# A fused attention and ELU feed-forward kernel: in the last step of a pair of heads, a copy of a product's bank goes ahead of the exponential

## The chip, the cores and the metric

The kernel runs on one core of one Trainium2 chip. The metric is the device time of one execution in microseconds. The kernel before was timed in six runs: median 1384.58 us, from 1382.22 to 1386.93. The engines are named as in the profile: PE is TensorE's matmul, PEld its weight load, DVE VectorE, ACT ScalarE, POOL GpSimd, SP SyncE, which issues the DMAs.

## The reference

Thresholded attention over 8 sequences, 8 heads, 576 positions of 64 values, in fp32, and then a feed-forward block with an ELU over the 4608 tokens.

```python
scores = scale * np.matmul(q, k.transpose(0, 1, 3, 2))          # (8, 8, 576, 576)
thresh = np.max(scores, axis=-1, keepdims=True) - tau
scores = np.where(scores >= thresh, scores, -1000000000.0)
attn = np.exp(scores - np.max(scores, axis=-1, keepdims=True))
attn = attn / (np.sum(attn, axis=-1, keepdims=True) + 1e-09)
x = np.matmul(attn, v)                                          # then to (4608, 512)
h = x @ w_in                                                    # (4608, 2048)
g = np.where(h > 0.0, h, np.exp(np.minimum(h, 0.0)) - 1.0)
out = g @ w_out                                                 # (4608, 512)
```

## The kernel before

The work is cut into 32 pairs of heads (8 sequences, 4 pairs each), and each pair into five steps. Steps 0 to 3 (`i < NC`, `NC` is 4) take 128 query rows of both heads; the fifth, `i == NC`, takes the last 64 rows of both heads together, as one set of 128 rows, so that it has a single score tile where the others have two. The attention of one sequence runs while the feed-forward products of an earlier one fill PE.

There are four stages. The first two attend the first sequence and the next pairs while weights are converted and a plain feed-forward runs. The third and longest is the loop at L1155 that this case is about: 115 steps, 23 pairs. What is left of the feed-forward runs after it with no attention beside it.

In the third stage the order on each engine is written out by an agenda: `at(t, f)` puts a job at a planned time `t`, `on_pe(cost, f)` runs all jobs that are due, then issues a piece of PE work and moves the planned clock on by its cost. The planned times are not run times; they only set the order in which instructions stand in each engine's queue. What waits for what is left to semaphores.

One step (`softmax`, L1115) starting at planned time `t`:

- scores (L238) on PE at once, one PSUM tile for each head, from two buffers;
- `max_of` (L1085, DVE) at `t + 1.2`: the row maximum `mx`;
- `bound_of` (L1089, POOL) at `t + 2.0`: the threshold `th`;
- `exp_of` (L1093 and L1095, both ACT) at `t + 2.1`: a scaled maximum `nb`, then the exponential `e`;
- `mask_of` (L1104, DVE): `e` where the score reaches the threshold, and the row sums; then the reciprocal (L1111, DVE) and the scaling of each head (L274, POOL);
- the transposition of the step before (L348 and L358, DVE, in 32 by 32 squares), which goes to DRAM and comes back two steps later by DMA (L361, L369);
- in steps 1 and 4, the product with the values of an earlier step (L384, L388, PE) and its copies (L395, L400, ACT).

Between these go quarters of the feed-forward (`ffn_quarters`). Both of its matrix products are done by a scheme with seven smaller products where eight would be plain. The first product (`first_product`, L846) has for one unit seven quarters `k = 0..6`, each of two fp32 matmuls, which the profile shows as four. They use three PSUM banks in turn, by `place`: `k = 0` and `3` and `6` write place 0, `k = 1` and `4` place 1, `k = 2` and `5` place 2. `k = 3`, `4`, `5` and `6` add to what is there. Between, ACT copies the banks out: after `k = 0`, `1` and `2` (L860) and after `k = 3` (L912) and `k = 4` (L913). L912 reads place 0, and `k = 6` then adds into place 0, so `k = 6` waits for L912. POOL adds some of the copies (L865), DVE adds the last two results to them (L868), and the ELU follows: an exponential on ACT (L879), minus one on ACT (L884) or POOL (L893), and DVE's L901. Four units make half a group; then the second product (`second_round`, L1001) reads the ELU's output and sums of it that POOL makes (L938).

A pair whose steps carry four units of the first product is followed by one that carries a second round: a round of the loop is two pairs, ten steps. In a first-product pair the fifth step is followed by the last four quarters (`k = 3..6`) of its fourth unit (`QUARTERS[4]` is `(4, 0)`). Line numbers up to L1122 are the same before and after the change.

Of the kernel before, what the change touches and what calls it, by code (L numbers as in the profile page):

```python
# [19 lines left out]
def kernel(  # L20
# [15 lines left out]
    NC = S // P  # L36
# [132 lines left out]
    def load(pr, parts=("qm", "km", "v"), shared=False):  # L169
        b, j = divmod(pr, NPAIR)  # L170
        tiles = raws.setdefault(pr, {})
        for name, src in (("qm", q), ("km", k)):
            if name not in parts:
                continue
            m = tiles[name] = raw.tile([P, S // T, T], FP32, name="qm" if shared else name)
            for i in range(2):
                for d in range(2):
                    r = (2 * i + d) * T
                    nc.sync.dma_start(
                        m[r : r + T],  # L180
                        src[b, 2 * j + i].rearrange("(j t) d -> t j d", t=T)[:, :, d * T : (d + 1) * T],
                    )
        if "v" not in parts:
            return
        vm = tiles["vm"] = raw.tile([P, 2, NC, D], FP32, name="vm", bufs=2)
        vd = tiles["vd"] = vds[pr % NVD]
        for i in range(2):
            vh = v[b, 2 * j + i]
            nc.sync.dma_start(vm[:, i], vh[:MAIN].rearrange("(c p) d -> p c d", p=P))
            r = slice(i * TAIL, (i + 1) * TAIL)  # L190
            nc.sync.dma_start(vd[r, r], vh[MAIN:])
# [30 lines left out]
    def scores(pr, i, hs):  # L222
        qT, kT, qd = pairs[pr]
        if hs[0] == 0:
            open_steps[pr, i] = {
                **{x: small.tile([P, 2], FP32, name=x) for x in ("mx", "nb", "th", "sm", "rs")},
            }
        st = open_steps[pr, i]
        if "f" in psum and not apart:
            both = psum["s"].tile([P, 2, 2, 512], FP32, name="sc")  # L230
            scs = {h: both[:, h] for h in hs}
        else:
            scs = {h: psum["s"].tile([P, 2, 512], FP32, name="sc") for h in hs}
        for a in range(2):
            for h in hs:
                k0 = a * HALF + (0 if h else TAIL)
                r, qs = (slice(h * D, (h + 1) * D), qT[:, i * P : (i + 1) * P]) if i < NC else (slice(0, P), qd)
                nc.tensor.matmul(scs[h][:, a, :HALF], qs[r], kT[r, k0 : k0 + HALF], start=True, stop=True)  # L238
        if len(hs) == 2 and not apart:
            st["both"] = both  # L240
        for h in hs:
            st[h] = scs[h]
# [27 lines left out]
    def normalize(pr, i, hs):  # L270
        st = open_steps[pr, i]
        for h in hs:
            wv = st["w"][:, h * S : (h + 1) * S]
            nc.gpsimd.tensor_scalar(wv, wv, st["rs"][:, h : h + 1], 1.0, ALU.mult, ALU.mult)  # L274
# [68 lines left out]
    def turn_squares(pr, i):  # L343
        w = open_steps.pop((pr, i))["w"]
        x = late["x"].tile([P, NT, NCH, T], FP32, name="x", bufs=2)

        def turn_part(c0, src, nc_):
            nc.vector.transpose(x[:, :, c0 : c0 + nc_], src.rearrange("p (c g n) -> p g c n", c=nc_, n=T))  # L348

        if i < NC:  # L350
            turn_part(0, w[:, :MAIN], NC)
            turn_part(NC, w[:, MAIN : MAIN + P], 1)
            turn_part(NC + 1, w[:, MAIN + P :], NC)
        else:
            turn_part(0, w[:, :MAIN], NC)
            turn_part(NC + 1, w[:, :MAIN], NC)
            for h in range(2):
                nc.vector.transpose(x[:, 2 * h : 2 * h + 2, NC], w[:, MAIN:S].rearrange("p (g n) -> p g n", n=T))  # L358
        there = turns[pr, i] = dram.tile([NT, T, NT, NCH * T], FP32, name="there")
        for p in range(NT):  # L360
            nc.sync.dma_start(  # L361
                there[:, :, p].rearrange("c k n -> k c n"), x[p * T : (p + 1) * T].rearrange("k c j n -> k c (j n)")
            )
# [48 lines left out]
    def run_extra(budget):  # L412
        while extra and extra[0][0] <= budget:
            cost, _, f = extra.popleft()
            budget -= cost
            f()
# [89 lines left out]
    def heads_of(i):  # L506
        return [0, 1] if i < NC else [0]
# [83 lines left out]
    with tc.manual_schedule():  # L591
# [3 lines left out]
        for n in range(per_seq, SWITCH):  # L595
            pr, i = step = steps[n]
# [149 lines left out]
    with tc.manual_schedule():  # L746
        after = []
        make_out(1), make_out(0)
        for n in range(SWITCH, MIDDLE):
            pr, i = steps[n]  # L750
# [46 lines left out]
        def at(t, f):  # L797
            serial[0] += 1
            heapq.heappush(agenda, (t, serial[0], f))
# [9 lines left out]
        def on_pe(cost, f):  # L809
            until(clock[0])  # L810
            f()
            clock[0] += cost
            return clock[0]
# [139 lines left out]
        def run_elus(t):  # L953
            while late_elus and late_elus[0][0] < t - 1.5:
                late_elus.pop(0)[1]()
# [127 lines left out]
        def max_of(pr, i, h):  # L1083
            st = open_steps[pr, i]
            nc.vector.tensor_reduce(st["mx"][:, h : h + 1], st[h][:, :, :HALF], axis=AX.XY, op=ALU.max)  # L1085

        def bound_of(pr, i, h):
            st = open_steps[pr, i]
            nc.gpsimd.tensor_scalar(st["th"][:, h : h + 1], st["mx"][:, h : h + 1], 1.0, ntau, ALU.mult, ALU.add)  # L1089

        def exp_of(pr, i, h):
            st = open_steps[pr, i]
            nc.scalar.mul(st["nb"][:, h : h + 1], st["mx"][:, h : h + 1], nkeep)  # L1093
            e = att.tile([P, 2, HALF], FP32, name="e")
            nc.scalar.activation(e, st[h][:, :, :HALF], AF.Exp, bias=st["nb"][:, h : h + 1], scale=keep)  # L1095
            st[h] = st[h], e

        def mask_of(pr, i, h):
            st = open_steps[pr, i]
            if h == 0:  # L1100
                st["w"] = wpool[0].tile([P, 2 * S], FP32, name="w")
            sc, e = st.pop(h)
            wv = st["w"][:, h * S : (h + 1) * S].rearrange("p (a n) -> p a n", a=2)
            nc.vector.scalar_tensor_tensor(wv, sc[:, :, :HALF], st["th"][:, h : h + 1], e, ALU.is_ge, ALU.mult,  # L1104
                                           accum_out=st["sm"][:, h : h + 1])

        def reciprocal_of(pr, i, hs):
            st = open_steps[pr, i]
            cs = slice(hs[0], hs[-1] + 1)
            nc.vector.tensor_scalar(st["sm"][:, cs], st["sm"][:, cs], 1e-9, None, ALU.add)  # L1110
            nc.vector.reciprocal(st["rs"][:, cs], st["sm"][:, cs])  # L1111
# [3 lines left out]
        def softmax(pr, i):  # L1115
            hs = heads_of(i)
            t = begun[0] = clock[0]
            on_pe(1.25, lambda: scores(pr, i, hs))
            turn_at = t + 1.25 + 0.72 * len(hs)
            for h in hs:  # L1120
                at(t + 1.2 + 0.01 * h, lambda h=h: max_of(pr, i, h))
                at(t + 2.0 + 0.75 * h, lambda h=h: bound_of(pr, i, h))  # L1122
                at(t + 2.1 + 1.05 * h, lambda h=h: exp_of(pr, i, h))
                at(turn_at + 1.6 + 0.85 * h, lambda h=h: mask_of(pr, i, h))
            if i or pr:
                at(turn_at, lambda: turn_squares(*steps[pr * NB + i - 1]))
            m = turn_at + 1.6 + 0.85 * len(hs)
            at(m, lambda: reciprocal_of(pr, i, hs))
            at(m + 0.1, lambda: run_elus(m))
            for h in hs:  # L1130
                at(m + 0.2 + 0.7 * h, lambda h=h: normalize(pr, i, [h]))
            for x in (2.8, 3.8, 5.0):
                at(t + x, lambda: run_extra(max(0.9, extra[0][0])) if extra else None)
            if pr + 1 < NP and i in (0, 2):
                at(m + 0.2, lambda: (prep_k if i else prep_q)(pr + 1))
                at(m + 1.3, lambda: (copy_k if i else copy_q)(pr + 1))

            if pr + 1 < NP and i == 0 and pr * NB > MIDDLE:
                at(m + 0.9, lambda: load(pr + 1, ("km",), True))
            if pr + 2 < NP and i == 2:  # L1140
                at(m + 0.9, lambda: load(pr + 2, ("qm",), True))
            if pr + 1 < NP and i == 3:
                at(m + 0.9, lambda: load(pr + 1, ("v",)))
# [11 lines left out]
        for n in range(MIDDLE, len(steps) + 3):  # L1155
            pr, i = divmod(n, NB)
# [116 lines left out]
```

## Time and profile before

| What | Value |
|---|---|
| median of six runs | 1384.58 us |
| the profiled execution: its time, its span | 1382.77 us, 1380.6 us |
| mean granted clock of TensorE | 0.992, and 1.00 in the loop |
| matmul PE, busy over the span | 97% |
| DVE, ACT, POOL, busy over the span | 77%, 45%, 60% |
| the third stage | about 316 to 1150 us |
| one round of it (ten steps) | 72.75 us |
| mean of one L1095, L912, L913 | 831, 364, 372 ns |
| mean of one L1085, L1104, L274 | 752, 811, 860 ns |

The profile is one execution. "Busy" of PE counts modelled ends of pipelined matmuls: matmuls that follow each other at 0.22 us are shown with some 0.38 us each. In a timeline, a row is a start and a duration in microseconds, the engine, the line, the operation, the tiles out and in, and the form; in brackets stand the idle time of the engine before it and what ended that. A wait list has who waited for whom: the sum in us, how often, and the longest.

### The profile page before, as it was taken

What the parts mean: (1) busy time and instruction counts of PE and PEld (TensorE: products, weight loads), DVE (VectorE), ACT (ScalarE), POOL (GpSimd) and SP (SyncE); (2) the same over time, 40 slices, a digit from 0 to 9 for tenths busy, and PEclk for the clock granted to TensorE, in tenths of its full rate; (3) what the DMA queues carried; (4) which work ended last, traced back from release to release, by engine and by line L of the source; (5) the groups of instructions that cost most, each with busy time, mean ns of one, the idle gap of its engine ahead of it and who ended that gap; (6) DMA issues with size and microseconds to landing.
All of it is one profiled execution on the core that took longest, in us unless ns stands there. A gap on an engine that the chain in (4) does not pass through costs nothing.

```text
span 1380.6 us, 21964 instructions
## 1 busy us (share of the span) xinstructions
PE 1334.5 (97%) x6566; PEld 990.1 (72%) x6566; DVE 1060.9 (77%) x2364; ACT 624.4 (45%) x1371; POOL 834.7 (60%) x1345
## 2 busy tenths in 40 slices
PE   6897989999999999999999999999999999999998
PEld 4454745747777777777777777777777777888886
DVE  6777885988878987888798878988888875545433
ACT  5665655325454544545353636364535452312320
POOL 5567774878647574757475747665575656525523
PEclk9999999999999999999999999999999999999999
DMA  5245452588898979898889888897889785321211
GB/s 115 58 87 147 139 148 44 183 246 245 233 264 224 269 215 252 220 257 236 244 228 258 243 227 245 217 262 214 233 234 279 211 246 168 122 69 61 97 57 31
DMA packets 316342, 259.82 MB, mean 188 GB/s; under 512 B 208320, under 2 KB 272320, under 8 KB 316224
## 3 DMA queue, kind: packets, MB, share of 16 engines
q1 hardware_dynamic: 316224, 258.42, 67.5%
q8 instruction: 53, 0.87, 0.3%
q14 instruction: 65, 0.53, 0.1%
HBM read 167.84 MB, written 90.51 MB: 187 GB/s over the span
## 4 chain that ended last, share of the span: by engine, by line
PE 71%; DVE 11%; ACT 5%; DMA 4%; POOL 4%; issue 3%; SPq 1%; DVEq 0%; POOLq 0%; ACTq 0%
PE f L1001 27%; PE f L846 19%; PE sc L238 10%; PE pv L388 8%; DMA there<-x 3%; PE pv L384 2%; PE f L435 2%; PE f L475 2%; DVE w L265 2%; DVE mx L1085 2%; ACT e L1095 2%; ACT e L253 1%; DVE x L348 1%; PE rt L277 1%; POOL wtop L143 1%
## 5 line engine op out<-in xcount | busy, mean ns | idle before, releaser
L274 POOL TENSOR_SCALAR w<-w,rs 128x576 f32<-128x576 f32 x288 | 246.2, 860 | 108.7 <-DVE rs L1111 75.2
L1085 DVE TENSOR_REDUCE mx<-sc 128x1 f32<-128x576 f32 x207 | 148.1, 752 | 82.8 <-PE sc L238 82.8
L238 PE MATMUL sc<-kT,qT 64*128 64x288 f32 x1024 | 182.6, 440 | 21.2 <-DVE w L265 11.6
L348 DVE STREAM_TRANSPOSE x<-w 128x512 f32<-128x512 f32 (+1 forms) x350 | 182.7, 568 | 8.2 <-POOL w L274 8.2
L1093 ACT ACTIVATE nb<-mx,nkeep 128x1 f32<-128x1 f32 x207 | 61.4, 297 | 253.3 <-DVE mx L1085 253.3
L1095 ACT ACTIVATE e<-sc,nb,keep 128x576 f32<-128x576 f32 x207 | 172.1, 831 | 7.0
L1104 DVE SCALAR_TENSOR_TENSOR w<-sc,th,e 128x576 f32<-128x576 f32 x207 | 163.2, 811 | 8.6 <-ACT e L1095 0.4
L238 PEld LDWEIGHTS sc<-kT,qT 64*128 64x128 f32 x1024 | 100.7, 191 | 86.1 <-issue 52.2
L846 PE MATMUL f<-xt,sw 128*128 128x256 f32 x512 | 128.9, 389 | 0.5 <-DVE g L868 0.5
L846 PE MATMUL f<-xt,w_in_sb 128*128 128x256 f32 x512 | 124.6, 382 | 0.3 <-ACT w L860 0.2
L1089 POOL TENSOR_SCALAR th<-mx,ntau 128x1 f32<-128x1 f32 x207 | 54.4, 264 | 111.9 <-DVE mx L1085 111.6
L846 PE MATMUL f<-x,w_in_sb 128*128 128x256 f32 x448 | 109.0, 382 | 5.5 <-ACT g L912 5.5
L846 PEld LDWEIGHTS f<-xt,sw 128*128 128x128 f32 x512 | 93.4, 190 | 28.9 <-issue 13.5
L253 ACT ACTIVATE e<-sc,nb,keep 128x576 f32<-128x576 f32 x81 | 65.1, 830 | 103.7 <-POOL nb L249 102.7
L846 PEld LDWEIGHTS f<-xt,w_in_sb 128*128 128x128 f32 x512 | 96.2, 190 | 18.8 <-ACT xs L400 4.6
L1001 PE MATMUL f<-w_out_sb,s 128*128 128x256 f32 x448 | 109.4, 387 | 0.0
L1001 PE MATMUL f<-w_out_sb,g 128*128 128x256 f32 x448 | 107.2, 382 | 0.0
L1001 PE MATMUL f<-t,s 128*128 128x256 f32 x448 | 106.6, 381 | 0.3 <-POOL s L938 0.3
L846 PEld LDWEIGHTS f<-x,w_in_sb 128*128 128x128 f32 x448 | 84.2, 190 | 21.1 <-ACT g L912 10.2
L1001 PEld LDWEIGHTS f<-w_out_sb,s 128*128 128x128 f32 x448 | 82.4, 190 | 22.9 <-issue 13.2
L1001 PEld LDWEIGHTS f<-w_out_sb,g 128*128 128x128 f32 x448 | 84.0, 190 | 15.8 <-ACT ge L879 2.7
L865 POOL TENSOR_TENSOR u<-u,w 128x256 f32<-128x256 f32 x64 | 48.9, 764 | 76.5 <-ACT u L860 76.5
(162 smaller groups left out, 2575.4 us busy)
## 6 DMA issues: line engine op xcount, KB each, us to landing
there<-x SPq DMA_DIRECT2D x500, 144.0 KB, 4.2
wTb<-there SPq DMA_DIRECT2D x75, 576.0 KB, 4.6
wTa<-there SPq DMA_DIRECT2D x50, 576.0 KB, 4.3
sw<-win_sums SPq DMA_DIRECT2D x62, 384.0 KB, 4.6
t<-wout_sums SPq DMA_DIRECT2D x45, 512.0 KB, 5.4
qm<-in_q_dram SPq DMA_DIRECT2D x128, 72.0 KB, 3.9
vm<-in_v_dram SPq DMA_DIRECT2D x64, 128.0 KB, 4.1
wst<-in_moe_w_in_dram SPq DMA_DIRECT2D x16, 512.0 KB, 4.6
```

The lines of the kernel that those rows point to most:

```text
L238: nc.tensor.matmul(scs[h][:, a, :HALF], qs[r], kT[r, k0 : k0 + HALF], start=True, stop=True)
L253: nc.scalar.activation(e, st[h][:, :, :HALF], AF.Exp, bias=st["nb"][:, h : h + 1], scale=keep)
L274: nc.gpsimd.tensor_scalar(wv, wv, st["rs"][:, h : h + 1], 1.0, ALU.mult, ALU.mult)
L348: nc.vector.transpose(x[:, :, c0 : c0 + nc_], src.rearrange("p (c g n) -> p g c n", c=nc_, n=T))
L388: nc.tensor.matmul(pv[h * D : (h + 1) * D, g0 * T : g1 * T], vm[:, h, c], wT[:, g0:g1, h * (NC + 1) + c], start=False, stop=(c == NC - 1), ...
L846: nc.tensor.matmul(loc["banks"][place], left[:, j], right[:, j], start=(begins and j == 0), stop=(j == 1), skip_group_check=True)
L1001: nc.tensor.matmul(place(m), lhs, rhs, start=(begins and v == 0), stop=(v == RU - 1), skip_group_check=True)
L1085: nc.vector.tensor_reduce(st["mx"][:, h : h + 1], st[h][:, :, :HALF], axis=AX.XY, op=ALU.max)
L1089: nc.gpsimd.tensor_scalar(st["th"][:, h : h + 1], st["mx"][:, h : h + 1], 1.0, ntau, ALU.mult, ALU.add)
L1093: nc.scalar.mul(st["nb"][:, h : h + 1], st["mx"][:, h : h + 1], nkeep)
L1095: nc.scalar.activation(e, st[h][:, :, :HALF], AF.Exp, bias=st["nb"][:, h : h + 1], scale=keep)
L1104: nc.vector.scalar_tensor_tensor(wv, sc[:, :, :HALF], st["th"][:, h : h + 1], e, ALU.is_ge, ALU.mult, accum_out=st["sm"][:, h : h + 1])
```

## The change

One planned time: in the fifth step of a pair the job that issues `nb` and the exponential is due 0.2 later, at `t + 2.3` where it was `t + 2.1`.

```diff
             for h in hs:
                 at(t + 1.2 + 0.01 * h, lambda h=h: max_of(pr, i, h))
                 at(t + 2.0 + 0.75 * h, lambda h=h: bound_of(pr, i, h))
-                at(t + 2.1 + 1.05 * h, lambda h=h: exp_of(pr, i, h))
+
+                at(t + (2.1 if i < NC else 2.3) + 1.05 * h, lambda h=h: exp_of(pr, i, h))
                 at(turn_at + 1.6 + 0.85 * h, lambda h=h: mask_of(pr, i, h))
```

The copy after `k = 3` is planned at the end of that quarter plus 0.1, which is `t + 1.25 + 0.87 + 0.1 = t + 2.22` when the four quarters are `k = 3..6`. So on ACT the copy L912 now comes before `nb` and the exponential of that step, where it came after them:

```
before: L1093 nb, L1095 e, L912 g, L913 g, L879 ge
after:  L912 g, L1093 nb, L1095 e, L913 g, L879 ge
```

Nothing else moves, and no instruction is added or removed.

## The prediction

> **What bounds the kernel now.** First the page, for the busy shares; then the stretches between one stall and the next; then the waits of TensorE (PE) in the main loop; then the chain of waits around one stall; last the timeline of that place.
>
> ```profile
> PE 1334.5 (97%) x6566; PEld 990.1 (72%) x6566; DVE 1060.9 (77%) x2364; ACT 624.4 (45%) x1371; POOL 834.7 (60%) x1345
> ...
> 494.26:567.00 72.74, 72.25 (x368) 54.47 (x368) 60.21 (x139) 35.34 (x81) 43.49 (x75) 1.00 0.85 232
> 567.00:639.75 72.75, 72.25 (x368) 54.48 (x369) 63.92 (x146) 34.60 (x79) 48.46 (x81) 1.00 0.88 246
> ...
> PE f L846 <- ACT g L912: 5.5, 11, 0.5
> ```
>
> In the stretches the columns are length, then busy time of PE, PEld (weight loads), DVE, ACT and POOL, the granted clock, the DMA share and GB/s. Between about 350 and 1149 us the program repeats every 72.75 us (ten steps, two pairs of heads), and PE is busy for 72.25 of it: the loop is bound by PE, and one gap of 0.5 us is left in each round. The wait list for 421.5 to 1149 us has that gap as its only PE entry: 11 times 0.5 us, always PE at L846 behind ScalarE's (ACT) copy L912. DVE has 9 to 12.5 us free in a round, POOL 24 to 29, ACT 37 to 38.
>
> ```profile
> 491.00 1.89 PE L846 MATMUL f<-xt,w_in_sb 128*128 128x256 f32 x8
> 492.01 0.75 DVE L1085 TENSOR_REDUCE mx<-sc 128x1 f32<-128x576 f32 x1
> 492.73 1.03 PE L846 MATMUL f<-x,w_in_sb 128*128 128x256 f32 x4
> 492.79 0.29 ACT L1093 ACTIVATE nb<-mx,nkeep 128x1 f32<-128x1 f32 x1 [1.99 <-DVE mx L1085]
> 493.11 0.83 ACT L1095 ACTIVATE e<-sc,nb,keep 128x576 f32<-128x576 f32 x1
> 493.85 0.36 ACT L912 COPY g<-f 128x256 f32<-128x256 f32 x1
> 494.10 0.38 ACT L913 COPY g<-f 128x256 f32<-128x256 f32 x1
> 494.26 0.73 PEld L846 LDWEIGHTS f<-x,w_in_sb 128*128 128x128 f32 x4 [0.91 <-ACT g L912]
> 494.26 1.13 PE L846 MATMUL f<-x,w_in_sb 128*128 128x256 f32 x4 [0.51 <-ACT g L912]
> 494.70 0.26 POOL L1089 TENSOR_SCALAR th<-mx,ntau 128x1 f32<-128x1 f32 x1
> 495.09 0.82 DVE L1104 SCALAR_TENSOR_TENSOR w<-sc,th,e 128x576 f32<-128x576 f32 x1
> ```
>
> One stall, read downward. The first row is products 4 and 5 (k=3 and k=4); eight matmuls take 1.89, so one follows the next by (1.89 - 0.38)/7 = 0.216, and k=3, the first four, ends at 491.00 + 3 x 0.216 + 0.38 = 492.03. The copy L912 reads its bank and could start then. ACT is idle from 490.79 to 492.79, but at the head of its queue stands nb (L1093), which waits for the row maximum on DVE (done at 492.76), then the exponential. So the copy starts at 493.85, 1.8 us late, and product 7 (k=6), which adds into the bank that is being copied, waits for it. The chain of waits agrees: between 492 and 494.3 us it runs mx, nb, e, L912, and only then PE.
>
> **What the Trainium skill says.** "TensorE: Matmul & The Clock Gate", section on the array's architectural detail: ACT and DVE are strict FIFO, while PE can pull weight loads ahead of running matmuls. Both show: L912 could run at 492.03 and sat behind L1093; and the load for k=5 leads its matmul by 0.22 us (492.51 against 492.73 in the timeline), while at the stall load and matmul start together at 494.26, so the load is no longer hidden. "PSUM — Partial Sum Buffer", section on bank collisions: a bank has to be guarded as a whole against two engines at once; that is why k=6 waits for the copy's end, as the eleven waits show. "Perfetto Trace Analysis", Optimization Strategy: look for the gap that repeats on the engine that should be saturated; here it is the 0.5 of every 72.75 us.
>
> **The change part by part.**
> 1. What moves. The program's order shows 12 places, all on ACT: L912 now stands before nb and the exponential of the fifth step. PE, DVE, POOL and SP keep every instruction in its place, so no DMA and no queue but ACT's is passed. It is 12 of the 23 fifth steps, those in pairs that run the first product; in the other eleven the order stays.
> 2. The copy. It becomes ready at 492.03 and takes 0.36: done about 492.41, inside the idle time of ACT, and product 7 can follow product 6 without a gap.
> 3. The exponential. What it adds is a wait in front of nb: L912 on PE's k=3. Queued behind are nb, the exponential and L913. But nb can't start before 492.76 anyway, 0.35 after the copy's end. So the exponential costs nothing more; its cover is the reduction L1085. Were that cover gone, the exponential would be later by at most the copy's 0.36, and its reader, the mask L1104, starts 1.15 us after the exponential's end (493.94 to 495.09), held by the threshold (494.96) and DVE's own queue.
> 4. L913 starts where L912 did, 0.25 earlier. Its reader on POOL (t, L865, at 495.61) waits for POOL's queue, which is full from 490.60 to 498.2. Gain nothing.
> 5. What one stall is worth. The two products take 494.26 + 1.13 - 492.73 = 2.66 us from start to end; unstalled, the same eight matmuls stand elsewhere in one row of 1.89 (L846 at 319.51). So 0.77 each, more than the 0.51 shown as idle: the row shows a modelled end, the pipeline restarts, and the weight load is exposed for 0.1.
> 6. The first of the twelve, at 347.20, is one row of 2.12: 0.23 to gain.
> 7. The last, at 1148.96, is different:
>
> ```profile
> 1152.33 2.03 PE L1001 MATMUL f<-w_out_sb,g 128*128 128x256 f32 x8
> 1152.91 0.69 DVE L901 SCALAR_TENSOR_TENSOR g<-ge,g 128x512 f32<-128x512 f32 x1 [0.31 <-ACT ge L884]
> 1153.65 0.30 PEld L1001 LDWEIGHTS f<-w_out_sb,g 128*128 128x128 f32 x2 [0.17 <-DVE g L901]
> ```
>
> There no scores stand between the values and the second product, and PE reaches the ELU of the last unit (L901, done 1153.60) just as it ends. That ELU hangs on POOL's full queue (t L865 at 1150.31), then DVE L868, ACT exp and minus, DVE L901: none of it moves. I take 0. In the ten others the same reader comes later, in the 498.80 row of L1001: after six of its matmuls, at 498.80 + 0.12 (the restart in a row of 2.00) + 6 x 0.216 = 500.2, against L901 done at 498.90. Of 1.30 us of slack 0.53 is left.
> 8. Sum: 10 x 0.77 + 0.23 + 0 = 7.9 us. Against the profiled execution (1382.77, its span 1380.6) that gives 1374.8; the median of the runs shown is 1384.58, 1.8 above it, and from there it is **1376.7**, my forecast.
>
> What is late next: with PE earlier by 0.77, DVE lags by that until it next waits for PE. After the stall at 421.51 its first idle times behind PE are 0.20 (433.26) and 0.74 (434.42), 0.94 in all: enough to take up 0.77, and from there DVE is driven by PE again. In the loop DVE waits 63.7 us for PE's scores in ten rounds, 6.4 in each. The tightest place left is this, in every second round:
>
> ```profile
> 442.73 0.73 POOL L938 TENSOR_TENSOR s<-s,g 128x256 f32<-128x256 f32 x1
> 443.50 0.73 PEld L1001 LDWEIGHTS f<-t,s 128*128 128x128 f32 x4 [0.18 <-POOL s L938]
> ```
>
> The sum s ends at 443.46 and the matmul that reads it starts at about 443.57. If POOL's sum moves with PE it costs nothing; if not, up to the whole 0.77. It is queued behind two thresholds that wait for maxima of scores from 439.70, and DVE was idle 0.36 for those scores: PE drives it, so I take nothing, and keep 5 x 0.77 = 3.9 for the range.
>
> **Rivals.**
> - Half is given back at that sum (every second round): gain 7.9 - 3.9 = 4.0, so 1380.6. For it: 0.1 us of slack. Against: the 0.36 above.
> - The gap moves: DVE and POOL, not PE, set the round, and PE waits 0.77 later in each for an ELU or a bank that DVE frees (L868, for which weight loads wait ten times, 3.2 us). Gain the 0.23 of the first at most: 1384.4. For it: DVE has 88% of a round like 567 to 639.75. Against: its 6.4 us of waiting for scores in each round.
> - Slower: DVE and POOL collide. The skill's "SBUF — State Buffer", on who interferes with whom, says that a DVE instruction with two inputs in SBUF, or in a two-port mode, contends with POOL's reads; in the trace POOL's scale L274 takes 0.73 alone and 1.17 beside DVE. The chain L865, L868, L879, L884, L901 feeds PE with 0.53 of slack left. New overlaps, from PE's new place, would have to lengthen it by over 1.30 to cost more than the stall did, three stretches of 0.44 in each round; with four (1.76) the loss is 0.46 x 10 = 4.6: 1389.2. Against: at that place DVE and POOL keep their order, and only what PE releases is shifted.
> - The copy holds up the exponential: it would need k=3 over 1.5 us (0.35 + 1.15) later than it ends now before the mask feels it. I give this nothing of its own.
>
> **How the numbers follow.** Forecast 0.66, half given back 0.16, the gap moves 0.12, slower 0.06. About 0.2% (2.8 us) is what a measurement of this kernel can tell from no change. The first two cases are faster by more: 0.82; the third is the same: 0.12; slower 0.06. Range: below, the forecast with the lower half of the spread of runs before (1382.22, 2.4 under the median) 1374.3; above, the case of half given back, 1380.6, with a little spread: 1381.2. That leaves 2 in 10 outside.
>
> **What would show it.** Right: the wait of PE for L912 gone from the list; L912 at about 1.0 us after the start of the row of k=3, with ACT idle before it behind PE; nb still released by mx; a round of 71.98 us instead of 72.75, with PE busy for all of it. Step 7 is right if PE waits for L901 near 1146 us for about 0.7. Wrong: a new PE entry of 0.3 to 0.8 in the list five or ten times (L938, L868 or L901), or an exponential that starts later after its scores than now and a mask that waits for it.

## The result, and the profile after

The changed kernel took 1375.91 us in the median of 16 runs; the kernel before, with the six runs shown above among 34, had a median of 1383.90. One of the 34, at 2291.86 us, is far from all others and is left out of the ratio, which compares mean times and so differs a little from that of the medians. The ratio is 0.9946, with a 95% interval from 0.9936 to 0.9956: about 7.5 us faster (6.1 to 8.9). The forecast was 1376.7, a gain of 7.9.

The wait list of PE over the third stage, 340 to 1149 us, of the kernel after (who waited for whom: sum in us, times, longest):

```profile
PE f L1001 <- DVE g L901: 0.5, 1, 0.5
```

One round from its stretches (length, then busy time of PE, PEld, DVE, ACT and POOL, clock, DMA share, GB/s):

```profile
493.20:565.20 72.00, 72.00 (x369) 54.59 (x368) 60.04 (x138) 35.36 (x81) 43.52 (x76) 1.00 0.86 235
```

The eleven waits for L912 are gone, and PE's busy time fills a round to the last digit. From the start of the row of k=3 at 490.20 to its like nine rounds later, at 1138.05, a round takes 71.98 us; before it took 72.75 (491.00 to 1145.71). The one new entry is at the very end of the stage.

The same place as the prediction shows, in the timeline after:

```profile
490.20 1.89 PE L846 MATMUL f<-xt,w_in_sb 128*128 128x256 f32 x8
...
491.20 0.74 DVE L1085 TENSOR_REDUCE mx<-sc 128x1 f32<-128x576 f32 x1
491.26 0.37 ACT L912 COPY g<-f 128x256 f32<-128x256 f32 x1 [1.27 <-PE f L846]
...
491.92 1.89 PE L846 MATMUL f<-x,w_in_sb 128*128 128x256 f32 x8
...
491.98 0.30 ACT L1093 ACTIVATE nb<-mx,nkeep 128x1 f32<-128x1 f32 x1 [0.35 <-DVE mx L1085]
492.31 0.83 ACT L1095 ACTIVATE e<-sc,nb,keep 128x576 f32<-128x576 f32 x1
...
493.65 0.59 PE L384 MATMUL pv<-wTa,vd 128*128 128x256 f32 x2
...
494.29 0.82 DVE L1104 SCALAR_TENSOR_TENSOR w<-sc,th,e 128x576 f32<-128x576 f32 x1
```

L912 now waits for PE, 1.06 after the start of the row of k=3, and is done before the maximum is. ACT then idles another 0.35 until DVE's maximum releases nb, so the exponential has not moved against the scores. The products k=5 and k=6 are one row of 1.89. The mask still starts 1.15 after the exponential's end. On PE these two products, from the start of k=5 to the start of the values (L384), are 1.73 us in every round, against 2.50 before (492.73 to 495.23): 0.77 a place. The row of the values before, which the prediction doesn't show:

```profile
495.23 0.59 PE L384 MATMUL pv<-wTa,vd 128*128 128x256 f32 x2
```

Of the 0.77, k=6 starts 0.67 earlier (2.59 after the start of the row of k=3, 3.26 before), and 0.10 is its row, 1.03 long without the stall and 1.13 with it.

The last of the twelve places, in the timeline after:

```profile
1143.90 1.56 PE L1001 MATMUL f<-w_out_sb,g 128*128 128x256 f32 x6
...
1145.26 0.69 DVE L901 SCALAR_TENSOR_TENSOR g<-ge,g 128x512 f32<-128x512 f32 x1 [0.31 <-ACT ge L884]
...
1146.00 0.70 PE L1001 MATMUL f<-w_out_sb,g 128*128 128x256 f32 x2 [0.54 <-DVE g L901]
```

Here the second product stops after six matmuls until the last ELU is done. With the restart and the exposed load this gives back the 0.77 that the copy had just gained: from the start of the row of k=3 to the next row of L1001 (`f<-t,g`) it is 8.49 us after the change (1138.05 to 1146.54) and was 8.48 before (1145.71 to 1154.19).

### The profile page after: what moved, and what is told of

Read it like the earlier page. It is cut to its first block, busy times and chain, and to the rows that moved or that the text cites. A ratio compares the mean times of both kernels' runs of the same rounds, so it can differ in the third digit from the quotient of the medians.

```text
span 1373.0 us, 21952 instructions
## 1 busy us (share of the span) xinstructions
PE 1330.9 (97%) x6566; PEld 991.3 (72%) x6566; DVE 1059.1 (77%) x2364; ACT 624.5 (45%) x1371; POOL 834.5 (61%) x1345
## 4 chain that ended last, share of the span: by engine, by line
PE 83%; DVE 7%; POOL 4%; ACT 2%; issue 2%; SPq 0%; DMA 0%; DVEq 0%; POOLq 0%; ACTq 0%
PE f L1001 28%; PE f L846 27%; PE sc L238 12%; PE pv L388 9%; PE pv L384 2%; PE f L435 2%; PE f L475 2%; DVE w L265 2%; ACT e L253 1%; PE rt L277 1%; POOL wtop L143 1%; POOL w L274 1%; DVE mx L248 1%; DVE wtop L137 1%; DVE wtop L136 1%
## 5 line engine op out<-in xcount | busy, mean ns | idle before, releaser
L1001 PE MATMUL f<-w_out_sb,s 128*128 128x256 f32 x448 | 109.4, 387 | 0.0
L1001 PE MATMUL f<-w_out_sb,g 128*128 128x256 f32 x448 | 107.6, 383 | 0.5 <-DVE g L901 0.5
L1001 PE MATMUL f<-t,s 128*128 128x256 f32 x448 | 106.7, 381 | 0.3 <-POOL s L938 0.3
L846 PE MATMUL f<-x,w_in_sb 128*128 128x256 f32 x448 | 105.9, 379 | 0.0
L1001 PEld LDWEIGHTS f<-w_out_sb,s 128*128 128x128 f32 x448 | 82.4, 190 | 22.9 <-issue 11.3
L1001 PEld LDWEIGHTS f<-w_out_sb,g 128*128 128x128 f32 x448 | 83.9, 190 | 16.8 <-issue 4.2
L1001 PEld LDWEIGHTS f<-t,s 128*128 128x128 f32 x448 | 84.2, 190 | 13.6 <-POOL s L938 2.7
```

The source lines that it names most:

```text
L846: nc.tensor.matmul(loc["banks"][place], left[:, j], right[:, j], start=(begins and j == 0), stop=(j == 1), skip_group_check=True)
L1001: nc.tensor.matmul(place(m), lhs, rhs, start=(begins and v == 0), stop=(v == RU - 1), skip_group_check=True)
```

## The experiments

Each was timed in turns with the kernel before on the same chip; ratios are to it. Line numbers in these kernels are two higher behind lines that were added.

### One place only: the last

```diff
-                at(t + 2.1 + 1.05 * h, lambda h=h: exp_of(pr, i, h))
+                at(t + (2.3 if (pr, i) == (NP - 1, NC) else 2.1) + 1.05 * h, lambda h=h: exp_of(pr, i, h))
```

> The copy goes ahead of the exponential in one place only, the fifth step of the last pair (the twelfth stall). Theory (the stall is removed, but the ELU that the second product reads hangs on POOL's full queue and does not move): no change, ratio 1.000 within 0.001. In the trace PE waits ten times for L912 (5.0 us) and once, newly, about 0.5 us for DVE's L901 some 4 us after the twelfth place. Rival (every removed stall is worth its 0.77 us): ratio 0.9994, no new wait for L901.

Measured: ratio 0.9993 (0.9984 to 1.0003). PE's wait list of this kernel, 340 to 1160 us:

```profile
PE f L846 <- ACT g L912: 5.0, 10, 0.5
PE f L1001 <- DVE g L901: 0.5, 1, 0.5
...
```

Ten waits stay, the twelfth place has none, and the wait for L901 has come in its stead. The time alone would also allow the rival's 0.9994; the new wait decides, and the rows of PE agree: from the row of k=3 to the row of `f<-t,g` it is 8.50 us here (1146.23 to 1154.73), 8.48 before. So a removed stall can be worth nothing, and this one is.

### The first six places

```diff
-                at(t + 2.1 + 1.05 * h, lambda h=h: exp_of(pr, i, h))
+                at(t + (2.3 if i == NC and pr < 20 else 2.1) + 1.05 * h, lambda h=h: exp_of(pr, i, h))
```

> The copy goes ahead in the first six of the twelve places. Theory (the gain is a sum over places, each about 0.76 us, none given back later in the loop): 6 x 0.75 = 4.5 us, ratio 0.9967; rounds of 71.98 us up to the sixth place and of 72.75 us after it. Rival (half comes back at the second product's sums in every second round): about 2.5 us, ratio 0.998, and waits for L938 in the list. Rival (the gain has another source than these places): a ratio far from half of the gain.

Measured: ratio 0.9974 (0.9961 to 0.9987). The interval holds both 0.9967 and the rival's 0.998, so the time does not decide between them. The timeline does: the rows of k=3 start 71.99 us apart from 417.96 to 705.91 (four rounds), and from there to 1141.71, six rounds, the mean is 72.63, which is one round of 71.99 (its stall is still removed) and five of 72.76. PE's list, 340 to 1160 us, has six waits for L912, 3.0 us, and besides one of 0.3 for a DMA and one of 0.3 for L938, past the end of the stage, that the kernel before has too (at 1158.96 there). Nothing is given back at that sum.

### The maximum earlier, ScalarE's order as before

This kernel has ScalarE's order of the kernel before. In step 3 of the odd pairs the ELUs are planned later, so that on DVE the maximum of the fifth step comes ahead of them.

```diff
-            at(m + 0.1, lambda: run_elus(m))
+            at(m + (1.7 if i == 3 and pr % 2 else 0.1), lambda: run_elus(m))
```

> ScalarE's order is that of the kernel before; instead DVE takes the maximum of the fifth step ahead of two ELUs (L901) that stood before it, so that nb and the exponential are done earlier. Theory (PE waits because the copy stands behind an exponential that is late, whatever makes it late): the maximum ends near 0.75 us after the scores, the exponential near 493.05 on the clock of the profile before, the copy near 493.4, before PE needs it at 493.6: the waits for L912 are gone or under 0.2 us, ratio 0.9946 to 0.9955. Rival (the gain comes from the exponential standing later or from what follows it in ScalarE's queue): no gain, ratio 1.000.

Measured: ratio 0.9954 (0.9937 to 0.9970), and no wait for L912. In PE's list, 340 to 1160 us, there is another instead:

```profile
PE f L1001 <- DVE g L901: 1.0, 2, 0.8
...
```

Its timeline:

```profile
494.13 1.89 PE L846 MATMUL f<-xt,w_in_sb 128*128 128x256 f32 x8
...
494.33 0.76 DVE L1085 TENSOR_REDUCE mx<-sc 128x1 f32<-128x576 f32 x1 [0.84 <-PE sc L238]
...
495.46 0.83 ACT L1095 ACTIVATE e<-sc,nb,keep 128x576 f32<-128x576 f32 x1
...
495.86 1.89 PE L846 MATMUL f<-x,w_in_sb 128*128 128x256 f32 x8
...
496.19 0.36 ACT L912 COPY g<-f 128x256 f32<-128x256 f32 x1
```

L912 stands behind the exponential as before, but is done at 496.55, before k=6 starts at 495.86 + 4 x 0.216 = 496.72. It is not the place of the copy that matters but when it is done. The stall had two causes that both were needed: the exponential ahead in the queue, and a maximum that stood 0.8 us in DVE's queue behind two ELUs. With the ELUs later, the mask starts 4.31 after the row of k=3 instead of 4.09, and PE waits for L901 0.8 at the last place instead of 0.5, and 0.2 once in the first round. In between, a round takes 72.00 us (494.13 to 1142.17 in nine).

### Both copies ahead

```diff
-                at(t + (2.1 if i < NC else 2.3) + 1.05 * h, lambda h=h: exp_of(pr, i, h))
+                at(t + (2.1 if i < NC else 3.2 if pr % 2 else 2.3) + 1.05 * h, lambda h=h: exp_of(pr, i, h))
```

> Both copies, L912 and L913, go ahead of nb and the exponential. L913 waits for PE's k=4, which ends about 0.1 us after the maximum, so the exponential is later by about 0.45 us than in the changed kernel. Theory (between the exponential's end and the mask lie 1.15 us): the mask does not move, ratio 0.9946 within 0.001, as the changed kernel. Rival (the exponential is on the path): about 0.45 us back in each of 12 places, ratio 0.9985; rival (an earlier L913 is what gains): ratio below 0.9935.

Measured: ratio 0.9942 (0.9926 to 0.9958), as the changed kernel. The interval reaches below 0.9935, so the time alone doesn't exclude that rival; the rounds do, with 71.98 us as in the changed kernel (492.49 to 1140.35 in nine).

```profile
495.01 0.83 ACT L1095 ACTIVATE e<-sc,nb,keep 128x576 f32<-128x576 f32 x1
...
496.56 0.82 DVE L1104 SCALAR_TENSOR_TENSOR w<-sc,th,e 128x576 f32<-128x576 f32 x1
```

The exponential starts 2.52 after the row of k=3 (495.01 to 492.49) instead of 2.11, so 0.41 later, and the mask at 4.07 instead of 4.09: it did not move. An L913 that starts 0.9 us earlier (1.92 after the row, 2.84 in the changed kernel) gains nothing.

### A later exponential, by a little and by much

Extra ScalarE instructions of one column, on a column that nothing reads, ahead of nb in the twelve places; three in the first kernel, eight in the second:

```diff
         def exp_of(pr, i, h):
             st = open_steps[pr, i]
+            for _ in range(3 if i == NC and pr % 2 else 0):
+                nc.scalar.mul(st["nb"][:, 1:2], tau_sb, nkeep)
             nc.scalar.mul(st["nb"][:, h : h + 1], st["mx"][:, h : h + 1], nkeep)
```

> The changed kernel, with three extra ScalarE instructions of one column ahead of nb in the twelve fifth steps: exponential and L913 are about 0.9 us later, L913 later than in the kernel before. Theory (slack of 1.15 us before the mask, and POOL's queue holds L913's reader anyway): no change against the changed kernel, ratio 0.9946 within 0.001. Rival (an earlier L913 is part of the gain): at least some of it is lost, ratio 0.996 or more.

Measured: ratio 0.9934 (0.9915 to 0.9953). The three took 0.95 us, part of it in ACT's idle time; exponential and L913 are 0.4 later than in the changed kernel, less than the 0.9 expected, and no time is lost: from 562.42 to 1138.29 a round takes 71.98 us. L913 is about where it stood in the kernel before against PE's row (3.24 after its start, 3.10 before): its earlier place is no part of the gain.

> The same with eight extra instructions, about 2.3 us. Theory: the exponential ends about 1.2 us after the mask could start; mask, L868 and L901 are later by about 1.2 us, and of the 0.53 us of slack before the second product reads that ELU nothing is left: PE waits for L901 about 0.7 us in each of the ten places and 1.7 us in the last, 8 to 9 us in all, ratio 1.000 to 1.002. Rival (there is more slack than that behind the mask): ratio below 0.997.

Measured: ratio 0.9982 (0.9973 to 0.9991), 3.6 thousandths, or 5.0 us, over the changed kernel's; 8 to 9 were expected. Its timeline:

```profile
570.63 0.83 ACT L1097 ACTIVATE e<-sc,nb,keep 128x576 f32<-128x576 f32 x1
...
571.56 0.82 DVE L1106 SCALAR_TENSOR_TENSOR w<-sc,th,e 128x576 f32<-128x576 f32 x1 [1.13 <-ACT e L1097]
571.80 0.73 POOL L865 TENSOR_TENSOR t<-g,u 128x256 f32<-128x256 f32 x1 [0.67 <-ACT g L913]
...
572.35 1.39 PE L238 MATMUL sc<-kT,qT 64*128 64x288 f32 x8
...
573.66 2.31 PE L1001 MATMUL f<-w_out_sb,g 128*128 128x256 f32 x8
...
575.27 0.30 PEld L1001 LDWEIGHTS f<-w_out_sb,g 128*128 128x128 f32 x2 [0.45 <-DVE g L901]
```

DVE now waits for the exponential, the weight load for L901, and two rows of PE are longer: the scores take 1.39 where they took 1.24, the eight matmuls that read the ELU 2.31 where they took 2.00. Together that is 0.46. The row of k=3 is at 566.49, so the exponential is 4.14 after it and 2.03 later than in the changed kernel, the mask 5.07 after it and 0.98 later. That leaves 1.05 us of room ahead of the mask: the 1.15 that was read off, less 0.1 from one instruction's end to the start of the one that it releases. A round takes 72.45 us (494.04 to 1146.07 in nine), 0.46 more. So the exponential does get on the path, through mask, L868 and L901 as was said, but at less cost than was sized: the first 0.4 of the extra work ran in ACT's idle time, and a place costs 0.46, not 0.7. The wait shows as longer rows and not as entries of PE's list, which has one wait for L901, of 1.4 at the last place. L913 is nearly on the path too: t now waits for it, and ends at 572.53, only 0.15 before L868 starts (572.68).

### The hold made longer

The kernel before, with two such instructions behind the exponential and ahead of L912.

```diff
             e = att.tile([P, 2, HALF], FP32, name="e")
             nc.scalar.activation(e, st[h][:, :, :HALF], AF.Exp, bias=st["nb"][:, h : h + 1], scale=keep)
+            for _ in range(2 if i == NC and pr % 2 else 0):
+                nc.scalar.mul(st["nb"][:, 1:2], tau_sb, nkeep)
```

> The kernel before, with two extra one-column instructions on ScalarE between the exponential and L912 in the twelve places. Theory (the copy's lateness is on PE's path one for one): each of the twelve stalls grows by what the two instructions take, about 0.55 us, 6 to 7 us in all, ratio 1.0045 to 1.005. Rival (other work takes up part of the stall): ratio 1.000 to 1.002.

Measured: ratio 1.0037 (1.0020 to 1.0054). PE's wait list, 340 to 1160 us:

```profile
PE f L846 <- ACT g L912: 11.5, 12, 1.0
...
```

The eleven waits grew from 0.5 to 1.0, the first of the twelve places now has one of 0.5, and a round from 72.75 to 73.25 us (496.11 to 1155.39 in nine, by the rows of k=5): 0.50 more wait, 0.50 more round. The stall is on PE's path one for one. The size, 12 x 0.5 = 6.0 us or 1.0043, is inside the interval.

### The last place: what holds that ELU

First POOL's two sums that stood ahead of t and of the scaling, put behind them in the last fifth step:

```diff
-            for x in (2.8, 3.8, 5.0):
+            for x in (2.8, 3.8, 5.0) if (pr, i) != (NP - 1, NC) else (5.0,):
```

> The changed kernel; in the last fifth step alone POOL's two sums (L938) that stood ahead of t (L865) and the scaling (L274) go behind. Theory (the last gap was turned into a wait for L901, which hangs on POOL's queue): t and L901 are 0.7 us earlier, PE no longer waits for L901, and the time is 0.5 to 0.8 us below the changed kernel's: ratio 0.9942. Rival (something else holds that ELU): the wait of 0.5 us stays.

Measured: ratio 0.9933 (0.9914 to 0.9952), not to be told from the changed kernel. The wait for L901 is still 0.5. Its timeline:

```profile
1142.39 0.73 POOL L865 TENSOR_TENSOR t<-g,u 128x256 f32<-128x256 f32 x1
...
1143.61 0.16 DVE L1111 RECIPROCAL rs<-sm 128x1 f32<-128x1 f32 x1
1143.69 0.42 DVE L868 TENSOR_TENSOR g<-f,t 128x256 f32<-128x256 f32 x1
...
1144.03 1.19 DVE L901 SCALAR_TENSOR_TENSOR g<-ge,g 128x512 f32<-128x512 f32 x1
...
1144.65 1.16 POOL L938 TENSOR_TENSOR s<-g,s 128x256 f32<-128x256 f32 x1
```

Against the row of k=3 (1138.48 here, 1138.05 in the changed kernel) t is 0.69 earlier, but L868 only 0.15: it now stands behind DVE's mask and reciprocal. And the ELU after it took 1.19 instead of 0.86. POOL's scaling had come forward with t (it runs from 1143.94 to 1144.68), so the ELU lies beside it and beside a sum, which takes 1.16 instead of 0.73. The theory that POOL's queue alone holds this ELU fell. The second kernel put mask and reciprocal of that step behind L868 and L901 as well:

```diff
-                at(turn_at + 1.6 + 0.85 * h, lambda h=h: mask_of(pr, i, h))
+                at(turn_at + (4.7 if (pr, i) == (NP - 1, NC) else 1.6) + 0.85 * h, lambda h=h: mask_of(pr, i, h))
...
-            m = turn_at + 1.6 + 0.85 * len(hs)
+            m = turn_at + (4.7 if (pr, i) == (NP - 1, NC) else 1.6) + 0.85 * len(hs)
...
-                at(clock[0], lambda: turn_squares(*steps[-1]))
+                at(clock[0] + 1.5, lambda: turn_squares(*steps[-1]))
```

> The changed kernel with the last fifth step's POOL sums behind t and scaling, as in the run before it, and now DVE's mask and reciprocal of that step behind L868 and the ELU L901 as well (the transposition of that step is planned 1.5 later). Theory (that ELU is held by two queues within 0.15 us of each other, POOL's up to t and DVE's through mask and reciprocal, so that both have to be cleared): L868 starts about 0.5 us earlier, L901 ends before PE comes for it, and the wait of 0.5 us for L901 is gone; the stage is 0.5 to 0.7 us shorter, ratio 0.994, too little to tell from the changed kernel by its time. Rival (the exponential and the minus one on ScalarE set it): the wait stays at 0.3 to 0.5 us.

Measured: ratio 0.9947 (0.9928 to 0.9965). The wait for L901 is gone from PE's list, and its only entry from 340 to 1160 us is another. In the timeline:

```profile
1145.41 0.42 DVE L868 TENSOR_TENSOR g<-f,t 128x256 f32<-128x256 f32 x1 [0.74 <-POOL t L865]
...
1148.00 0.30 PEld L1001 LDWEIGHTS f<-w_out_sb,g 128*128 128x128 f32 x2 [0.26 <-DVE g L901]
...
1154.52 1.13 PE L1001 MATMUL f<-t,s 128*128 128x256 f32 x4 [1.50 <-POOL s L938]
```

L868 waits for t alone again, and the weight load is held 0.26 instead of 0.94. So both queues held the ELU, 0.15 us apart. But the postponed scaling and sums come late in their turn, and PE waits 1.5 us for L938 a little later. As an improvement it fails; neither of the two kernels is better than the change in a way that the runs can tell.

## Why the prediction was right

Point by point, by its own steps.

Steps 1 to 3, the order and the copy, held to a few hundredths: L912 runs in ACT's idle time behind PE, nb is still released by the maximum 0.35 later. That the exponential has cover is shown by the two kernels that delay it: by 0.4 it costs nothing, by 2.0 it costs 0.46 a round.

Step 4, nothing to gain from L913, is shown by the kernel with both copies ahead.

Step 5, the price of 0.77 for a wait that the list shows as 0.5, was exact: 72.75 to 71.98, by its own parts (a modelled end that hid 0.16 of the gap, a load exposed for 0.10). Reading the sum off the wait list, 5.5 us, would have fallen short by a quarter.

Step 6: the first place is worth 0.23 from the order, as the kernel with only the last place changed shows, where it is still one row of 2.12 and the values start 1.96 after k=5 begins. In the profile of the kernel before the values start another 0.49 later there, behind a wait that the profile puts down to a DMA; in the kernel with three extra instructions and in the one with the sums moved the same place waits 0.9 to 1.0 us for one, with no stall ahead. The kernel with only the last place changed has the order of the kernel before up to there and shows no such wait; the one with the last sums moved has the order of the changed kernel, which shows none either. So it comes and goes between executions and is not the change's.

Step 7: that the last place is worth nothing was right, and shown twice; the wait near 1146 us was put at about 0.7 and shows as 0.54. Its reason was half right: POOL's queue was not the only one that held the ELU.

Step 8, the sum of 7.9, lies in the interval of 6.1 to 8.9. In the two profiled executions the rounds account for it: eleven places from k=5 at 347.20 to k=5 at 1147.43 took 800.23 us, after the change 791.94 (347.83 to 1139.77), 8.3 less, of which 0.49 is that DMA's. The spans differ by 7.6, since the execution after reached the third stage 0.6 us later.

The tightest place left, the sum L938 in every second round, moved with PE, as was taken: no wait for it in the list, and rounds that are all alike. The rivals of half the gain, of the moved gap and of the collision have no trace in the loop. Longer instructions on DVE and POOL did show where work was shifted, in the kernel with the last sums moved: the ELU by 0.33 us.

Two readings of the prediction don't hold as they stand. The 63.7 us that DVE waits for scores come from 421.5 to 1076 us, which is nine rounds and not ten: 7.1 in each, not 6.4, which speaks more strongly against the moved gap. And that k=6 waits for L912 needs no rule on banks: it adds into the place that L912 copies out, so the data alone ask for the wait, and no run parts the two.

## What to carry to other kernels

When the engine that sets the time waits for a short copy, look at what stands ahead of the copy in its own engine's queue and what that is waiting for: an instruction that isn't ready yet can let a ready one pass at no cost, as long as its own release comes later than the copy's end. Price a gap between pipelined matmuls from start to start of the work around it, not from the idle time that is shown. And ask at each removed wait whether the next operand is there: of twelve equal edits the last bought nothing.

## What the runs showed that was not expected

In the kernel with the last sums moved an ELU instruction on DVE took 1.19 us instead of 0.86, and a sum on POOL beside it 1.16 instead of 0.73. The Trainium skill's "SBUF — State Buffer", on who interferes with whom, says that a DVE instruction with two SBUF inputs contends with POOL's reads. The ELU has two and the sum reads two, so this case agrees; no run was made to show it as the cause. And a late mask costs PE in two places: at the ELU, and already at the next scores (1.39 us instead of 1.24). Those need the PSUM tile that the mask reads: in the kernel with eight extra instructions their second matmul starts at 572.53, after the mask's end at 572.38.
